# A fused attention and two MLPs on one core: the fixed order of the first batch written anew

## The chip, the cores and the metric

The kernel runs on one core of a Trainium2 chip. The metric is the device time of one execution in microseconds (us). "Before" is the kernel as it stood, "after" the kernel with the change.

## What is computed

The reference is an attention over pooled keys and values, and two MLPs behind it, all in float32:

```python
# q, k, v: (8, 8, 576, 64) = batch, heads, sequence, head size
k_p = k.reshape(B, H, 72, 8, D).mean(axis=3)      # 576 rows pooled to 72
v_p = v.reshape(B, H, 72, 8, D).mean(axis=3)
scores = scale * q @ k_p.T ; attn = softmax(scores)
x = (attn @ v_p) -> (4608, 512)                   # batch*sequence, heads*D
h = x @ w_in1 ; x = max(0.01*h, h) @ w_out1       # 512 -> 2048 -> 512
h = x @ w_in2 ; r = max(h, 0) ; out = (r*r) @ w_out2
```

The weights arrive as 64-bit floats, and the kernel decodes them itself from pairs of 32-bit words.

## The kernel before, in words

**Stages.** The first MLP runs over tiles of 512 tokens (`WIDE`, five of them) and 16 slices of 128 hidden columns; for each unit (tile t, slice f) `first` makes h = w_in^T x on PE and the activation, and `second` adds w_out^T g into four PSUM accumulators. Every operand of a product is split into a high and a low part (`hi` by a cast on ACT, `lo` by a subtraction on DVE), and three products take the place of one (`three`, lines 317 to 319). Behind that both MLPs go on in a scheme with fewer products (`first2`, `second2`), which the change does not touch.

**Attention beside the MLP.** `attention()` is a generator. Batch 0 is written out by hand in `first_batch`, since nothing can run beside it: the first MLP waits for its result. The other seven batches are stepped by `advance()`, some 2.5 steps a unit in the first tile and 5.25 later, so that they lie between the MLP's products.

**One batch.** The keys of 8 heads are loaded as 512 rows a head (`load_main`, 64 x 512 numbers a DMA; two tiles of 128 partitions, k_0 and k_2) and 64 more rows (`load_rest`, rk). `pooled` adds the 8 rows of a pool on DVE (line 356) or, for the batches in `K_ON_PE` and `V_ON_PE`, `pooled_pe` lets PE add them by products with the identity matrix (line 365: kp for keys, vp for values). `prepare_k` transposes the pooled keys on PE and copies them, scaled, into kT (ACT). `prepare_v` makes the values vM (high part on ACT, low part on DVE) and a block vR of the remaining rows, by way of GpSimd and six small DMAs (rx). The queries come in five chunks of up to 128 tokens, at 0, 128, 256 (64 wide), 320 and 448. For each chunk: `stage_a` transposes the queries (trq, PE) and copies them (qT, ACT). `stage_parts` makes the scores s (PE, line 554), their maxima mx (DVE, 564), eight exponentials x (ACT, 571), the sums' reciprocals rs (DVE, 584) and the products p (GpSimd, 586 and 593). `keys_part` and `rest_part` transpose p (pt, pr on PE), and `stage_d` makes the products o with the values, whose halves xh and xl are the MLP's input.

**Weights.** `fetch_weights` loads one slice (512 KB of w_in, 512 KB of w_out) into one of two staging buffers. `decode` turns it into floats in steps that share one buffer m: for slices 0 and 1 three operations on DVE (lines 205, 209, 212), one that puts in the sign (216), and a last one (226, an addition) that also waits for ACT's copy of the low words (225). For later slices ACT does the first (207). `split_weights` makes hl, high (ACT, 244) and low (DVE, 245).

**What sets the order.** In `first_batch` the lines q_in, a, b, c1, c2, d, w, fetch and next(pk), next(pv) emit the steps in the order in which each engine shall run them, and `in_order` fixes that order on each engine: no instruction there can pass the one ahead of it on its engine. a(i) is `stage_a` of chunk i; b(i) the next of the four parts of `stage_parts`; c1 and c2 are `keys_part` and `rest_part`; d(0) and d(4) one step of `stage_d` for the first 320 and the last 256 tokens; w(f) one step of decoding slice f. Behind h(0,0) the order is a scheduler's.

**Loads before.** ACT issues the four DMAs of k_0; SP issues rk, k_2, the queries of chunks 0 and 1, rv, the eight DMAs of the values, the queries of chunks 2 to 4, weight slice 0, rx, weight slice 1, and the queries and keys of batch 1.

**PSUM.** Four banks (`ps_w`) go round for trk, trq, vp, kp, pt, pr, o and h; the scores of batch 0 take the four banks of `ps_a` that are the MLP's accumulators later.

## Time and profile before

| | us |
|---|---|
| median of 3 runs (lowest, highest) | 1641.63 (1640.09, 1642.88) |
| the profiled execution | 1641.07 |
| its span, first to last instruction | 1639.3 |
| PE busy, share of the span | 1602.6, 98% |
| DVE busy | 1388.1, 85% |
| ACT busy | 1008.1, 61% |
| POOL busy | 117.3, 7% |

How to read the profile: PE is TensorE (PEld its loading of weights), DVE is VectorE, ACT ScalarE, POOL GpSimd, SP the engine that issues most DMAs; SPq and ACTq are issues of DMAs. Times count from the span's first instruction. A row of a timeline gives start, busy time, engine, line of the kernel, operation, "out<-in", and how often (x4); in brackets stands how long the engine was idle before it, and what ended that. A product of two float32 operands that are not split appears as two records.

### The profile page before, as it was taken

The numbers are of one execution on the slowest core, as the hardware profiler recorded it, in microseconds if no ns is written. First come the engines' busy times: TensorE is split into PE (matmuls) and PEld (weight loads), VectorE is DVE, ScalarE is ACT, GpSimd is POOL, SyncE is SP. The second block draws the span as 40 slices with busy tenths as digits, with TensorE's granted clock in tenths as the row PEclk, the third lists the DMA queues.
The fourth block names the chain that finished last, engine by engine and source line by source line (L and its number), as shares of the span: only waits on it lengthen the run. The fifth ranks groups of instructions, "written<-read, shape, count | busy, mean of one in ns | idle before, by whom it ended". The sixth has DMA issues, their size and how long they took to land.

```text
span 1639.3 us, 25990 instructions
## 1 busy us (share of the span) xinstructions
PE 1602.6 (98%) x9032; PEld 1466.8 (89%) x9032; DVE 1388.1 (85%) x2070; ACT 1008.1 (61%) x1930; POOL 117.3 (7%) x149
## 2 busy tenths in 40 slices
PE   5999999999999999999999999999999999999999
PEld 4877788888888999999999999998998998998997
DVE  6899776789889999979759589889789799799687
ACT  6777677755667867667557547456456455465454
POOL 4121222223110000000000000000000000000000
PEclk9999999999999999999999999999999999999999
DMA  8675554777547688887766764865865756756655
GB/s 212 190 203 169 144 134 139 233 217 224 180 157 257 244 284 296 265 304 231 225 190 204 236 186 151 281 196 149 275 187 176 254 177 198 241 171 209 196 167 167
DMA packets 223730, 340.94 MB, mean 208 GB/s; under 512 B 56176, under 2 KB 138096, under 8 KB 223600
## 3 DMA queue, kind: packets, MB, share of 16 engines
q1 hardware_dynamic: 223280, 338.76, 66.3%
q8 instruction: 72, 1.18, 0.3%
q10 hardware_dynamic: 320, 0.52, 0.1%
q14 instruction: 58, 0.48, 0.1%
HBM read 268.44 MB, written 69.21 MB: 206 GB/s over the span
## 4 chain that ended last, share of the span: by engine, by line
PE 83%; DVE 8%; ACT 4%; DMA 3%; issue 1%; SPq 0%; POOL 0%; ACTq 0%; DVEq 0%; POOLq 0%
PE psum L1078 14%; PE psum L317 14%; PE psum L319 14%; PE psum L318 14%; PE psum L1079 7%; PE h L317 3%; PE h L319 3%; PE h L318 3%; PE acc L318 3%; PE acc L319 2%; PE acc L317 2%; PE s L554 1%; ACT x L571 1%; DMA xs<-x 1%; DVE hl_out L245 1%
## 5 line engine op out<-in xcount | busy, mean ns | idle before, releaser
L1078 PE MATMUL psum<-wb_out,oh 128*128 128x512 f32 x1008 | 352.8, 394 | 0.0
L317 PE MATMUL psum<-xh,wb_in 128*128 128x384 f32 x1008 | 337.3, 335 | 2.2 <-ACT s L1052 1.2
L319 PE MATMUL psum<-xh,wb_in 128*128 128x384 f32 x1008 | 336.8, 334 | 0.0
L318 PE MATMUL psum<-xl,wb_in 128*128 128x384 f32 x1008 | 336.8, 334 | 0.0
L930 ACT CAST oh<-g 128x768 fp32r<-128x768 f32 x252 | 210.3, 836 | 160.1 <-PE psum L1078 89.3
L1079 PE MATMUL psum<-wb_out,ol 128*128 128x256 f32 x1008 | 281.8, 280 | 0.0
L931 DVE TENSOR_TENSOR ol<-g,oh 128x768 fp32r<-128x768 f32 x252 | 239.4, 954 | 17.4 <-ACT oh L930 14.9
L1078 PEld LDWEIGHTS psum<-wb_out,oh 128*128 128x128 f32 x1008 | 189.6, 188 | 43.1
L317 PEld LDWEIGHTS psum<-xh,wb_in 128*128 128x128 f32 x1008 | 189.2, 188 | 3.9 <-ACT s L1052 1.5
L318 PEld LDWEIGHTS psum<-xl,wb_in 128*128 128x128 f32 x1008 | 189.2, 188 | 0.2
L319 PEld LDWEIGHTS psum<-xh,wb_in 128*128 128x128 f32 x1008 | 189.2, 188 | 0.0
L1079 PEld LDWEIGHTS psum<-wb_out,ol 128*128 128x128 f32 x1008 | 188.8, 187 | 0.2
L984 ACT CAST wb_in<-wb_in 128x512 fp32r<-128x512 f32 x144 | 89.3, 621 | 146.4 <-DMA wb_in<-ws_in 141.4
L985 DVE TENSOR_TENSOR wb_in<-wb_in 128x512 fp32r<-128x512 f32 x144 | 98.7, 688 | 80.3 <-ACT wb_in L984 79.8
L934 DVE TENSOR_TENSOR g<-g,g 128x768 f32<-128x768 f32 x144 | 136.0, 952 | 1.5 <-ACT g L1006 1.0
L317 PE MATMUL h<-xh,hl_in 128*128 128x512 f32 (+1 forms) x320 | 121.8, 381 | 4.0 <-DVE pt_r L619 2.8
L317 PE MATMUL acc<-gh,hl_out 128*128 128x512 f32 (+1 forms) x320 | 120.2, 382 | 1.4 <-ACT hl_out L244 1.1
L318 PE MATMUL acc<-gl,hl_out 128*128 128x512 f32 (+1 forms) x320 | 118.6, 373 | 0.7 <-DVE gl L865 0.7
L319 PE MATMUL h<-xh,hl_in 128*128 128x512 f32 (+1 forms) x320 | 118.7, 371 | 0.0
L318 PE MATMUL h<-xl,hl_in 128*128 128x512 f32 (+1 forms) x320 | 118.1, 369 | 0.0
L319 PE MATMUL acc<-gh,hl_out 128*128 128x512 f32 (+1 forms) x320 | 117.9, 371 | 0.0
L318 PE MATMUL psum<-ol,wb_out 128*128 128x384 f32 x336 | 112.6, 335 | 0.0
(161 smaller groups left out, 3113.7 us busy)
## 6 DMA issues: line engine op xcount, KB each, us to landing
wb_in<-wd_in SPq DMA_DIRECT2D x108, 512.0 KB
wb_out<-wd_out SPq DMA_DIRECT2D x108, 512.0 KB
wb_in<-ws_in SPq DMA_DIRECT2D x144, 256.0 KB
wb_out<-ws_out SPq DMA_DIRECT2D x144, 256.0 KB
xs<-x SPq DMA_DIRECT2D x18, 768.0 KB
out_dram<-o SPq DMA_DIRECT2D x23, 384.0 KB
q<-in_q_dram SPq DMA_DIRECT2D x32, 256.0 KB
v<-in_v_dram SPq DMA_DIRECT2D x64, 128.0 KB
```

What stands on the lines that cost most here:

```text
L245: nc.vector.tensor_tensor(out=lo, in0=w, in1=raw(hi), op=ALU.subtract)
L317: nc.tensor.matmul(outp, ah, bh, start=first, stop=False, **kw)
L318: nc.tensor.matmul(outp, ah, bl, start=False, stop=False, **kw)
L319: nc.tensor.matmul(outp, al, bh, start=False, stop=last, **kw)
L554: nc.tensor.matmul(sc[:n, 2 * m:2 * m + 2].rearrange("p a x -> p (a x)"), qT[:, 2 * e + m, :n], kT[b % 2][:, 2 * e + m].rearrange("p a x - ...
L930: nc.scalar.copy(hi, src)
L931: nc.vector.tensor_tensor(out=lo, in0=src, in1=raw(hi), op=ALU.subtract)
L934: nc.vector.tensor_tensor(out=out_, in0=a, in1=b, op=ALU.subtract)
L984: nc.scalar.copy(whole[:, 0], raw(whole[:, 1]))
L985: nc.vector.tensor_tensor(out=whole[:, 1], in0=raw(whole[:, 1]), in1=raw(whole[:, 0]), op=ALU.subtract)
L1078: nc.tensor.matmul(outp, ah, b, start=first, stop=False, skip_group_check=True)
L1079: nc.tensor.matmul(outp[:, 1], al, b[:, 0], start=False, stop=last, skip_group_check=True)
```

## The change

- The first loads go over both issuing engines. ACT: both DMAs of the first half of the keys (`load_first`, 64 x 2 x 512 numbers each), the queries of chunks 0 and 1, both of the first half of the values. SP: the rest of the keys, the second half of the keys, weight slice 0, the rest and the second half of the values, the queries of chunks 2 to 4.
- The values of batch 0 are pooled by PE (vp) instead of DVE.
- The keys of batch 1 are loaded earlier, and their pooling by PE (kp) moves from behind h(0,0) to ahead of it; one PSUM bank stays with kp until ACT copies it, behind h(0,0).
- The decoding of weight slice 0 and most of slice 1 moves ahead of parts of the attention.
- The transposes and copies of the first keys are made half by half.
- For the batches from 1 on, the pooling of the last rows of keys (`pool_rest`) stands behind kp.

```diff
--- before.py
+++ after.py
@@ -56,7 +56,7 @@
     RG = KR * H // 2
     SPANS = (320, 256)
     EARLY = 5
-    V_ON_PE = (1,)
+    V_ON_PE = (0, 1)
     K_ON_PE = (1,)
     AHEAD = 5
     RATES = (2.5, 5.25)
...
+            def load_first(src, nm, issue):
+
+                ts = []
+                for g in range(2):
+                    ts.append(kv_tile(0, P, 2, f"{nm}0_{g}"))
+                    heads = src[0, 4 * g:4 * g + 4, 0:KM * POOL, :].rearrange(
+                        f"({'a r' if nm == 'k' else 'r a'}) (kk j) d -> a kk r (j d)", a=2, j=POOL
+                    )
+                    for a in ((0, 1), (1, 0))[g]:
+                        issue[g].dma_start(out=ts[g][a * KM:(a + 1) * KM], in_=heads[a])
+                return ts
+
+            def load_rest(b, src, nm):
...
             def load_k(b):
-                if b < B:
-                    both = [nc.scalar, nc.sync] if b == 0 else [nc.sync, nc.sync]
+                if b == 0:
+                    KV["k", b] = load_rest(b, k, "k"), load_first(k, "k", [nc.scalar, nc.sync])
+                elif b < B:
                     KV["k", b] = (
-                        load_rest(b, k, "k", both[1]),
-                        load_main(
-                            b, k, "k", [[4 * (m // 2) + m % 2 + 2 * a for a in range(2)] for m in range(NP)], both
-                        ),
+                        load_rest(b, k, "k"),
+                        load_main(b, k, "k", [[4 * (m // 2) + m % 2 + 2 * a for a in range(2)] for m in range(NP)]),
                     )
 
             def load_v(b):
+                if b == 0:
+                    KV["v", b] = load_rest(b, v, "v"), load_first(v, "v", [nc.scalar, nc.sync])
+                    return
                 KV["v", b] = (
                     load_rest(b, v, "v"),
...
             def prepare_k(b):
                 kr, kk = KV.pop(("k", b))
                 i = b % 2
                 kd = ap1.tile([P, NP, D], F32, tag="kd", name=f"kd{b}")
                 rr = ap1.tile([KR * H, 2, D], F32, tag="rr", name=f"rr{b}")
-                pooled(rr[:, 0:1], kr)
-                nc.vector.tensor_copy(rr[:, 1], rr[:, 0])
+
+                def pool_rest():
+                    pooled(rr[:, 0:1], kr)
+                    nc.vector.tensor_copy(rr[:, 1], rr[:, 0])
+
+                if b == 0:
+                    pool_rest()
+                    tr = work("trk0")
+                    for g in range(2):
+                        pooled(kd[:, 2 * g:2 * g + 2], kk[g])
+                        turned(tr, kd, g)
+                        if g == 0:
+                            turned_rest(tr, rr)
+                            put_rest(i, tr)
+                        put_keys(i, tr, slice(2 * g, 2 * g + 2))
...
+                    return
                 if b in K_ON_PE:
                     for ps in pooled_pe(f"kp{b}", kk):
                         yield
+                    pool_rest()
                     nc.scalar.copy(kd, ps)
                 else:
+                    pool_rest()
                     for m in range(0, NP, 2):
                         pooled(kd[:, m:m + 2], kk[m // 2])
-                        if b > 0:
-                            yield
-                            continue
-                        tr = work("trk0") if m == 0 else tr
-                        nc.tensor.transpose(
-                            tr[:, m * D:(m + 2) * D], kd[:, m:m + 2].rearrange("p a d -> p (a d)"), ident
-                        )
                         yield
-                if b > 0:
-                    load_v(b)
-                    tr = work(f"trk{b}")
-                for g in range(2 if b > 0 else 0):
-                    nc.tensor.transpose(
-                        tr[:, g * P:(g + 1) * P], kd[:, 2 * g:2 * g + 2].rearrange("p a d -> p (a d)"), ident
-                    )
-                nc.tensor.transpose(
-                    tr[:, 2 * P:2 * P + KR * H], rr.rearrange("p a d -> p (a d)"), ident[:KR * H, :KR * H]
-                )
-                for r in range(2):
-                    rows = slice(r * D, (r + 1) * D)
-                    nc.scalar.activation(
-                        kT[i][rows, :, r, 0:KM], tr[rows, 0:2 * P].rearrange("p (m x) -> p m x", x=KM),
-                        AF.Copy, scale=scale / POOL,
-                    )
-                    nc.scalar.activation(
-                        kT[i][rows, :, r, KM:SP],
-                        tr[rows, 2 * P:2 * P + KR * H].rearrange("p (m r x) -> p m r x", r=2, x=KR)[:, :, r],
-                        AF.Copy, scale=scale / POOL,
-                    )
...
-            def load_q(b, span, at, off, n):
+            def load_q(b, span, at, off, n, issue=None):
                 qn[b, at] = qp.tile([P, H, D], F32, tag="q", name=f"q{b}_{at}", bufs=3)
-                nc.sync.dma_start(out=qn[b, at][:n], in_=q[b, :, at:at + n, :].rearrange("h p d -> p h d"))
...
+            pk1 = []
+
             def first_batch():
-                pk, pv = prepare_k(0), prepare_v(0)
...
                     stage_a(*chunks[i])
@@ -696,78 +737,81 @@
                     RAW[f] = fetch_weights(1, [("in", f), ("out", f)])
 
                 load_k(0)
-                q_in(0)
-                q_in(1)
+                q_in(0, nc.scalar)
+                q_in(1, nc.scalar)
+                fetch(0)
                 load_v(0)
+                pk, pv = prepare_k(0), prepare_v(0)
                 q_in(2)
                 next(pk)
                 a(0)
                 next(pk)
-                next(pk)
                 a(1)
                 q_in(3)
                 q_in(4)
-                fetch(0)
-                next(pv)
-                fetch(1)
                 b(0)
                 b(0)
                 b(1)
+                next(pv)
+                fetch(1)
+                load_k(1)
+                pk1.append(prepare_k(1))
+                b(0)
+                b(1)
+                w(0)
+                w(0)
+                next(pv)
+                next(pv)
+                a(2)
                 b(1)
                 b(0)
-                next(pv)
-                b(1)
-                b(0)
-                a(2)
-                next(pv)
-                b(1)
-                a(3)
+                w(0)
                 b(2)
                 b(2)
                 next(pv)
+                a(3)
                 b(2)
-                b(2)
-                c1(0)
+                b(1)
+                w(0)
                 b(3)
                 b(3)
+                c1(0)
                 c2(0)
+                b(3)
+                b(2)
+                a(4)
+                b(4)
+                b(4)
                 c1(1)
                 c2(1)
                 next(pv)
-                a(4)
+                b(4)
+                b(3)
+                w(1)
+                w(1)
+                split_weights("in", 0, 0)
+                fetch(2)
+                c1(2)
+                c2(2)
+                b(4)
+                next(pk1[0])
+                d(0)
+                d(0)
+                d(0)
+                d(0)
+                w(1)
                 q_in(5)
                 q_in(6)
                 q_in(7)
-                load_k(1)
-                c1(2)
-                c2(2)
-                b(3)
-                b(4)
-                b(4)
-                w(0)
-                b(3)
-                d(0)
-                d(0)
-                b(4)
-                w(0)
-                b(4)
-                d(0)
-                d(0)
-                w(0)
-                w(0)
-                fetch(2)
                 c1(3)
                 c2(3)
+                next(pk1[0])
                 c1(4)
                 c2(4)
-                split_weights("in", 0, 0)
-                w(1)
-                w(1)
                 d(4)
                 d(4)
                 d(4)
                 d(4)
-                w(1)
                 w(1)
                 first(0, 0)
                 fetch(3)
@@ -783,7 +827,7 @@
             marks.append(in_order(first_batch))
             ready[0] = 1
             yield
-            yield from prepare_k(1)
+            yield from pk1[0]
             stage_b(*chunks[nch])
             yield
             def finish(i):
```

Where the order moves, on the engines that the prediction speaks of. In these rows a name ends in the chunk's first token and a running number; s, mx, x, qT, trq are the scores, maxima, exponentials and transposed queries of a chunk.

ACT, from the first exponentials on, before:

```order
L571 ACTIVATE x_0_279,sm_0_280<-s_0_0_282,mx_0_0_288 128x72 x4
L571 ACTIVATE x_0_279,sm_0_280<-s_0_1_285,mx_0_1_290 128x72 x4
L571 ACTIVATE x_128_292,sm_128_293<-s_128_0_295,mx_128_0_301 128x72 x4
L571 ACTIVATE x_128_292,sm_128_293<-s_128_1_298,mx_128_1_303 128x72 x4
L537 COPY qT_256_335<-trq_256_330 128x4x64
L537 COPY qT_320_351<-trq_320_346 128x512
L500 ACTIVATE vM_181<-vd_262 64x4x64 x2
```

and after:

```order
L611 ACTIVATE x_0_256,sm_0_257<-s_0_0_259,mx_0_0_265 128x72 x4
L611 ACTIVATE x_0_256,sm_0_257<-s_0_1_262,mx_0_1_267 128x72 x4
L577 COPY qT_256_345<-trq_256_340 128x4x64
L611 ACTIVATE x_128_269,sm_128_270<-s_128_0_272,mx_128_0_314 128x72 x4
L611 ACTIVATE x_128_269,sm_128_270<-s_128_1_275,mx_128_1_316 128x72 x4
L540 ACTIVATE vM_181<-vp_323 64x4x64 x2
L577 COPY qT_320_384<-trq_320_379 128x512
L611 ACTIVATE x_256_362,sm_256_363<-s_256_0_365,mx_256_0_371 64x72 x4
L611 ACTIVATE x_256_362,sm_256_363<-s_256_1_368,mx_256_1_373 64x72 x4
L225 ACTIVATE w_0_318<-st_in_out_203 128x1024
L645 CAST pt_h<-pt_0_415 128x4x128
```

The copy qT_256 has moved between the exponentials of chunks 0 and 1, qT_320 stays behind them and behind vM, which is now made from vp; the copy for weight slice 0 (w_0) comes ahead of pt_h.

PE, behind the scores of chunks 0 and 1, before (trq_256 is the transposes of q_256):

```order
L554 MATMUL s_0_1_285<-kT_179,qT_0_237 128x144 x2
L554 MATMUL s_128_0_295<-kT_179,qT_128_253 128x144 x2
L554 MATMUL s_128_1_298<-kT_179,qT_128_253 128x144 x2
L533 MATMUL trq_256_330<-ident,q_256_219 128x64 x4
L533 MATMUL trq_320_346<-ident,q_320_255 128x128 x4
L554 MATMUL s_256_0_356<-kT_179,qT_256_335 64x144 x2
```

and after:

```order
L594 MATMUL s_128_0_272<-kT_179,qT_128_250 128x144 x2
L594 MATMUL s_128_1_275<-kT_179,qT_128_250 128x144 x2
L365 MATMUL vp_323<-v_0_208,ident 128x128 x8
L365 MATMUL vp_323<-v_1_211,ident 128x128 x8
L573 MATMUL trq_256_340<-ident,q_256_214 128x64 x4
L594 MATMUL s_256_0_365<-kT_179,qT_256_345 64x144 x2
```

The pooling of the values, vp, stands between the scores and trq_256.

PE, ahead of the last products of the attention (o_1), after; before, kp stands behind the first products of h_0_1 instead:

```order
L678 MATMUL o_0_3_550<-pt_r,vR 128x320
L644 MATMUL pt_320_564<-ident,p_320_485 128x128 x4
L656 MATMUL pr_320_571<-ident,p_320_485 96x128 x2
L365 MATMUL kp_520<-k_2_301,ident 128x128 x8
L644 MATMUL pt_448_584<-ident,p_448_514 128x128 x4
L656 MATMUL pr_448_591<-ident,p_448_514 96x128 x2
L317 MATMUL o_1_0_596<-pt_h,vM_181 128x256
```

The second half of kp stands ahead of the transposes pt_448.

DVE, around the last decode step of slice 3 and the first of slice 4, behind h(0,0), before:

```order
L216 SCALAR_TENSOR_TENSOR wm_3_666<-st_in_out_634,wm_3_666 128x1024
L356 TENSOR_TENSOR rr_710<-rk_436 64x64
L226 ISA w_3_665<-wm_3_666,w_3_665 128x2048
L428 COPY rr_710<-rr_710 64x64
L209 TENSOR_SCALAR wm_4_677<-wm_4_677 128x1024
L212 TENSOR_SCALAR wm_4_677<-wm_4_677 128x1024
L356 TENSOR_TENSOR rv_749<-rv_749 64x256
```

and after (rv, rd and mx belong to batch 1):

```order
L216 SCALAR_TENSOR_TENSOR wm_3_689<-st_in_out_657,wm_3_689 128x1024
L474 COPY rr_519<-rr_519 64x64
L356 TENSOR_TENSOR rv_737<-rv_737 64x256
L226 ISA w_3_688<-wm_3_689,w_3_688 128x2048
L356 TENSOR_TENSOR rv_737<-rv_737 64x128
L604 TENSOR_REDUCE mx_0_0_782<-s_0_0_776 128x4
L356 TENSOR_TENSOR rd_884<-rv_737 64x64
L604 TENSOR_REDUCE mx_0_1_784<-s_0_1_779 128x4
L209 TENSOR_SCALAR wm_4_700<-wm_4_700 128x1024
```

The rest of the second values and the first maxima of batch 1 have come ahead of L209 of slice 4.

## Rows read from the trace of the kernel before

**Rows 1.** The page, part 1: engine, busy us (share of the span), instructions.

```profile
PE 1602.6 (98%) x9032; PEld 1466.8 (89%) x9032; DVE 1388.1 (85%) x2070; ACT 1008.1 (61%) x1930; POOL 117.3 (7%) x149
```

**Rows 2.** Windows: stretch, length, PE, PEld, DVE, ACT, POOL busy, PEclk, DMA share, GB/s.

```profile
0.00:5.00 5.00, 0.00 (x0) 0.00 (x0) 0.38 (x1) 1.49 (x2) 4.34 (x13) 1.00 0.50 139
5.00:10.00 5.00, 0.58 (x3) 0.61 (x4) 2.82 (x9) 0.00 (x0) 0.00 (x0) 1.00 1.04 226
10.00:15.00 5.00, 4.86 (x20) 3.76 (x19) 2.04 (x7) 2.60 (x9) 1.26 (x1) 1.00 0.84 221
15.00:20.00 5.00, 3.06 (x18) 2.48 (x18) 3.84 (x10) 5.00 (x32) 0.80 (x1) 1.00 1.15 282
20.00:25.00 5.00, 5.00 (x28) 4.34 (x26) 3.78 (x10) 3.80 (x20) 3.48 (x6) 0.66 0.90 274
...
40.00:45.00 5.00, 4.95 (x20) 4.47 (x21) 4.87 (x10) 2.66 (x9) 0.00 (x0) 0.61 0.35 118
```

**Rows 3.** Timeline of ACT, 14 to 22 us.

```profile
14.49 0.32 ACT L571 ACTIVATE x<-s,mx 128x72 f32<-128x72 f32 x1 [1.34 <-DVE mx L564]
...
19.25 0.95 ACT L537 COPY qT<-trq 128x256 f32<-128x256 f32 x2
...
21.35 0.85 ACT L500 ACTIVATE vM<-vd 64x256 fp32r<-64x256 f32 x2 [1.15 <-DVE vd L356]
```

**Rows 4.** Timeline of PE, the last products o_1 and the first of h(0,0).

```profile
42.76 0.41 PE L318 MATMUL o<-pt_l,vM 128*128 128x256 f32 x1
42.98 0.41 PE L319 MATMUL o<-pt_h,vM 128*128 128x256 f32 x1
...
43.64 0.63 PE L317 MATMUL h<-xh,hl_in 128*128 128x512 f32 x1
```

**Rows 5.** Windows behind h(0,0), and the longest wait of PE in them.

```profile
44.00:76.00 32.00, 30.59 (x175) 25.17 (x175) 28.60 (x45) 25.06 (x54) 1.66 (x2) 1.00 0.66 198
76.00:110.00 34.00, 31.23 (x158) 25.34 (x156) 32.95 (x54) 27.43 (x70) 9.15 (x10) 1.00 0.75 218
110.00:152.00 42.00, 39.03 (x191) 31.55 (x191) 41.27 (x63) 32.78 (x79) 7.40 (x7) 1.00 0.58 168
...
92.79 0.47 PE L317 MATMUL h<-xh,hl_in 128*128 128x512 f32 x1 [2.77 <-DVE pt_r L619]
```

**Rows 6.** Timeline of SP's issues: weight slice 0.

```profile
15.07 0.83 SPq L191 DMA_DIRECT2D st_in_out<-in_moe_w_in_dram  x1
15.95 0.50 SPq L196 DMA_DIRECT2D st_in_out<-in_moe_w_out_dram  x1
```

**Rows 7.** Timeline of PE, transposes of queries and scores.

```profile
11.41 1.11 PE L533 MATMUL trq<-ident,q 128*128 128x128 f32 x4
12.66 4.14 PE L554 MATMUL s<-kT,qT 128*128 128x144 f32 x16
16.73 0.46 PE L533 MATMUL trq<-ident,q 64*128 64x64 f32 x4
17.52 0.63 PE L533 MATMUL trq<-ident,q 128*128 128x128 f32 x4 [0.32 <-DMA q<-in_q_dram]
```

**Rows 8.** Timeline of PE, pooling by products: half of kp, all of vp, batch 1.

```profile
56.03 1.95 PE L365 MATMUL kp<-k,ident 128*128 128x128 f32 x16
...
72.87 3.84 PE L365 MATMUL vp<-v,ident 128*128 128x128 f32 x32 [0.43 <-ACT x L571]
```

**Rows 9.** Timeline of DVE: decode steps of slices 0 and 4.

```profile
36.96 1.23 DVE L226 CUSTOM_DVE_ANT_0 w<-wm,w 128x2048 uint16<-128x2048 uint16 x1
...
61.55 0.69 DVE L209 TENSOR_SCALAR wm<-wm 128x1024 f32<-128x1024 f32 x1 [1.10 <-ACT wm L207]
```

**Rows 10.** DMA queues between 2 and 6 us: packets, MB, share (q10 is ACT's).

```profile
q10 hardware_dynamic: 298, 0.49, 42.6%
q1 hardware_dynamic: 266, 0.46, 42.4%
```

More of the change, by code (lines that the diff above doesn't have):

```diff
@@ L418, in load_v, with turned, turned_rest, put_keys @@
                 )
+            def turned(tr, kd, g):
+                nc.tensor.transpose(
+                    tr[:, g * P:(g + 1) * P], kd[:, 2 * g:2 * g + 2].rearrange("p a d -> p (a d)"), ident
+                )
+            def turned_rest(tr, rr):
+                nc.tensor.transpose(
+                    tr[:, 2 * P:2 * P + KR * H], rr.rearrange("p a d -> p (a d)"), ident[:KR * H, :KR * H]
+                )
+            def put_keys(i, tr, ms):
+                for r in range(2):
+                    rows = slice(r * D, (r + 1) * D)
+                    nc.scalar.activation(
+                        kT[i][rows, ms, r, 0:KM], tr[rows, 0:2 * P].rearrange("p (m x) -> p m x", x=KM)[:, ms],
+                        AF.Copy, scale=scale / POOL,
+                    )
+            def put_rest(i, tr):
+                for r in range(2):
+                    rows = slice(r * D, (r + 1) * D)
+                    nc.scalar.activation(
+                        kT[i][rows, :, r, KM:SP],
+                        tr[rows, 2 * P:2 * P + KR * H].rearrange("p (m r x) -> p m r x", r=2, x=KR)[:, :, r],
+                        AF.Copy, scale=scale / POOL,
+                    )
             def prepare_k(b):
@@ L660, in attention, with q_in @@
             nch = len(chunks) // B
+            pk1 = []
             def first_batch():
-                pk, pv = prepare_k(0), prepare_v(0)
                 part = [None] * nch
                 dec, rows = {}, {}
-                def q_in(i):
-                    load_q(*chunks[i])
+                def q_in(i, issue=None):
+                    load_q(*chunks[i], issue)
                 def a(i):
```

17 lines of the change are left out of this document (12 added, 5 removed).

## Prediction

> **What bounds the kernel now.** I read the page first, then the windows, the timelines of ACT, PE, SP and DVE over the first 50 us, and the windows behind them. PE is busy 98% of the span and DVE 85% [rows 1], so a part of the program can only gain where PE does not already work without a break, and that is the beginning. In the first 25 us the DMA engines are what works: their share is 1.04, 0.84, 1.15 and 0.90 in the four windows from 5 us on, and only the first window, at 0.50, has room [rows 2]. ACT takes over from there. It starts on the exponentials of chunk 0 at 14.49 and has finished those of chunks 0 and 1 when it copies qT_256 and qT_320 at 19.25, so 16 exponentials with their read-outs take 4.76 us, 2.38 a chunk. At 20.20 both copies are done, and at 21.35 ACT has waited 1.15 us for the pooled values [rows 3]. The first MLP product, h(0,0), starts on PE at 43.64 [rows 4]. From there to about 152 us DVE is the tight engine: 28.60 of 32, 32.95 of 34 and 41.27 of 42 us, while PE leaves 1.4, 2.8 and 3.0 us idle and once waits 2.77 us for a DVE result [rows 5]. What moves the end is therefore the start of h(0,0), and behind it DVE's work.
>
> **The sum goes against the profiled execution's 1641.07 us**, which is 0.56 below the median of the runs shown, 1641.63; 0.2% is 3.3 us, about what a measurement of this kernel can tell from no change.
>
> **Step 1, the loads.** The megabyte of weight slice 0 (two issues of 512 KB, 0.83 and 0.50 us of SP's time [rows 6]) moves from behind q_448 to ahead of the last 64 rows and of half of the values. Everything behind it on SP, that is rv, v_1 and q_256 to q_448, lands later. I count bytes at the rates of the first windows [rows 2]: 0.70, 1.83, 2.93 and 4.34 MB have moved by 5, 10, 15 and 20 us. The values need 0.13 + 1.05 + 0.52 + 0.13 + 1.05 = 2.88 MB before the change (rest of the keys, keys, q_0 and q_128, rest of the values, values) and 3.93 MB after it, which is 15 + 1.00 / 0.282 = 18.5 us. Before, DVE could take the values at 17 us without a wait. A landing is later than the count: q_320 is due at 16.2 by it (3.28 MB) and PE waits for it until 17.52 [rows 7], 1.3 us more. I take 0.7, so v_1 at 19.2, with 18.5 and 19.8 as ends.
>
> That the loads go over two queues I price at nothing. By the windows alone [rows 2] a second queue could at most fill the first 5 us to the rate of the next 5: (226 - 139) x 5 us = 0.43 MB, or 1.6 us less of lag; from 5 us on no DMA time is free. I take none of it, since the first window also holds the start, when nothing has been issued yet. The Trainium skill has a rule on this in "DMA: Bandwidth & Descriptors", section "Issuing engines are not separate DMA queues": transfers started by different engines run on the same 16 DMA engines, and a second issuer saves only the time of issuing. By that rule the gain is nothing as well, where the row's upper end is 1.6 us.
>
> **Step 2, what waits for them.** In the new PE order the pooling of the first values (vp) stands ahead of the transposes trq_256, and in ACT's order qT_256 still stands ahead of the exponentials of chunk 1. So a late v_1 holds back q_256, and through it ACT, with everything that ACT has queued. The 32 records of one vp take 3.84 us [rows 8]; the second half, 16, comes behind v_1: 19.2 + 1.92 = 21.1. The transposes take 0.46 [rows 7], the copy 0.48 (half of 0.95 [rows 3]): 22.05. The exponentials of chunk 1 take 2.38: 24.4; qT_320, which is not yet copied then, 0.48: 24.9. Before, the same state is reached at 20.20. **Lag: 4.7 us.** Low end 4.0, with v_1 at 18.5. High end 6.8: v_1 at 19.8 and PE at the slower of its levels, at which four transposes took 1.11 instead of 0.63 [rows 7], so 3.4 for the half vp. The second values issue on ACT sits ahead of the first kT copies; it costs one issue (0.5 to 0.8 [rows 6]) in a stretch where ACT waits for q_0 anyway: nothing.
>
> **Step 3, from there to h(0,0).** ACT has the same operations in both orders, so only waits count. The 1.15 us for the values on ACT [rows 3] go, since vp is then long done. The last 16 products of the attention (o_1) ran at a granted clock of 0.61 in their window [rows 2], one per 0.22 us [rows 4], the pace of 1.2 GHz; with the key pooling kp ahead of them PE has work there, and at 2.4 GHz the 16 take half of their 3.5 us: -1.75. Against it, the second half of kp, 16 records and 1.95 us [rows 8], stands ahead of pt_448 in PE's queue, and every later product waits for that: +1.95 (0 if PE would have waited for GpSimd there anyway). And the maxima of chunk 320 now stand in DVE's queue behind the last decode step of slice 0 (1.23 us [rows 9]), which waits for ACT's copy: +1.2 (0 if ACT gets there early). -1.15 - 1.75 + 1.95 + 1.2 = **+0.25**; ends -2.9 and +3.15.
>
> **Step 4, behind h(0,0).** kp's 32 records leave the MLP's stretch: 3.9 us less for PE. I count that at nothing, because DVE is the tight engine there: PE's wait of 2.77 us for DVE [rows 5] becomes longer by what PE saves. DVE's own work behind h(0,0) stays: the decode step of slice 1 that now comes earlier ends in a wait for the first gl. What PE's lead buys is that DVE finds the rest of the second values and the first maxima of batch 1 ready where it waited 1.10 us for ACT [rows 9]: **-1.1**, with 0 as the other end. Pooling the first values on PE takes two v poolings from DVE, in the stretch where ACT is the bound: nothing.
>
> 4.7 + 0.25 - 1.1 = +3.85 us: 1644.9 on the profiled execution, **1645.5** against the median. The forecast's own range is 1642.5 to 1649.
>
> **Rivals.**
> *The weights starve the small pieces* (slower still). While both queues move pieces of 2 KB they share evenly, 298 packets of one and 266 of the other between 2 and 6 us [rows 10]. q_0 and q_128 come in pieces of 256 bytes and would meet the weights' pieces of 1 and 4 KB. If the queues take turns by piece, SP's queue is through before q_128 is: 3.41 MB, 16.7 + 0.7 = 17.4 us. Then the chain from q_128's transposes to the last score, 11.41 to 16.80 [rows 7], ends at 22.8, vp at 26.6, qT_256 at 27.6, and with 2.86 more the state of 20.20 comes at 30.4: lag 10.2, so 1651. The skill's same page, section "Queues, rings and completion order", says that an engine goes round its queues packet by packet, which would be this case; with equal pieces [rows 10] it can't be told from sharing by bytes. Chance 0.15.
>
> *PE counts behind h(0,0)*. If DVE's order, not its amount of work, makes PE's waits there [rows 5], PE's 3.9 us come off: 1641.6. For it: PE is busy 30.59 of 32 us in the first of these windows. Against it: DVE is nearly without a gap in the next two. Chance 0.17.
>
> *The loads are not late* (faster). The first 5 us have a DMA share of 0.50 [rows 2]; four large issues in place of eight could fill it. It decides if v_1 is there by 14.5 us, so that half a vp and the transposes are done when chunk 0's exponentials end at 16.9. Then there is no lag, slice 0 is decoded early, kp hides in waits for GpSimd: -2.9 - 1.1 = -4.0, 1637.6. Against it: a full first window gives the 1.6 us of step 1, not 4.7; it would need a fuller use later too. Chance 0.20.
>
> **How the numbers follow.** The forecast has 0.48. Faster by over 0.2% means under 1638.4: most of the third rival and a little of the second, 0.17. Slower by over 0.2% means over 1644.9: more than half of the forecast's range, the first rival, 0.46. The rest, 0.37. The range runs from 1638.4, which leaves out the better part of the third rival, to 1650.5.
>
> **What would show it.** Right: ACT waits 3 us or more ahead of qT_256; trq_256 comes after 20 us, behind vp, whose second half waits for a DMA; h(0,0) starts near 48.5; PE's idle time between h(0,0) and 110 us behind it grows by about kp's 3.9 us; the granted clock is 1.00 in the window of o_1. Wrong: exponentials of chunk 0 after 17 us (first rival); h(0,0) at 48.5, yet a time near 1641 (second); qT_256 before 18 us and h(0,0) before 43 (third).

## The result, and the profile after

| | before | after |
|---|---|---|
| median, us (4 runs each, same chip) | 1642.26 | 1665.38 |
| lowest, highest | 1640.09, 1644.78 | 1662.40, 1666.34 |
| the profiled execution, its span | 1641.07, 1639.3 | 1664.83, 1663.1 |
| start of h(0,0) in the profile | 43.64 | 64.41 |
| from there to the end of the span | 1595.7 | 1598.7 |

The ratio is 1.0137, 95% interval [1.0117, 1.0157]: some 22 us slower. Of the 23.8 us between the two profiles 20.8 lie ahead of h(0,0) and 3.0 behind it.

The page of after, part 1, and the windows of the beginning (columns as in [rows 1, 2]):

```profile
PE 1612.4 (97%) x9064; PEld 1478.0 (89%) x9064; DVE 1383.1 (83%) x2064; ACT 1008.7 (61%) x1932; POOL 117.6 (7%) x149
```
```profile
0.00:5.00 5.00, 0.00 (x0) 0.00 (x0) 0.00 (x0) 0.00 (x0) 4.36 (x13) 1.00 0.53 117
5.00:10.00 5.00, 0.74 (x2) 0.36 (x2) 2.51 (x7) 0.51 (x1) 0.00 (x0) 1.00 1.17 170
10.00:15.00 5.00, 1.45 (x5) 0.90 (x5) 1.41 (x3) 2.26 (x7) 0.00 (x0) 1.00 1.13 290
15.00:20.00 5.00, 0.15 (x1) 0.00 (x0) 0.00 (x0) 0.72 (x3) 0.00 (x0) 1.00 1.07 193
20.00:25.00 5.00, 4.19 (x20) 4.20 (x21) 1.52 (x4) 2.18 (x12) 0.00 (x0) 1.00 0.67 147
...
45.00:50.00 5.00, 4.86 (x25) 4.27 (x24) 3.85 (x7) 4.63 (x22) 2.62 (x3) 0.50 0.38 60
50.00:55.00 5.00, 3.26 (x13) 2.91 (x13) 3.55 (x8) 0.72 (x3) 3.00 (x5) 0.50 0.01 2
55.00:60.00 5.00, 5.00 (x30) 4.94 (x29) 3.56 (x6) 1.93 (x5) 0.12 (x1) 0.64 0.00 0
60.00:65.00 5.00, 4.21 (x28) 3.34 (x27) 2.24 (x6) 2.50 (x10) 0.00 (x0) 1.00 0.06 13
```

From 15 to 20 us, where ACT had no gap before, every engine nearly stands (ACT 0.72 us busy, PE 0.15) and the transfers run at a share of 1.07. The timelines of ACT, then of PE, show what stood for what (they answer to [rows 3, 4, 7, 8]):

```profile
23.41 0.32 ACT L611 ACTIVATE x<-s,mx 128x72 f32<-128x72 f32 x1 [0.87 <-DVE mx L604]
...
29.26 0.37 ACT L577 COPY qT<-trq 128x256 f32<-128x256 f32 x1 [3.32 <-PE trq L573]
...
33.26 0.59 ACT L577 COPY qT<-trq 128x512 f32<-128x512 f32 x1
...
39.13 0.32 ACT L611 ACTIVATE x<-s,mx 128x72 f32<-128x72 f32 x1 [1.13 <-DVE mx L604]
...
41.52 0.62 ACT L577 COPY qT<-trq 128x512 f32<-128x512 f32 x1
45.37 0.59 ACT L645 CAST pt_h<-pt 128x512 fp32r<-128x512 f32 x1 [3.23 <-PE pt L644]
```
```profile
12.97 1.12 PE L573 MATMUL trq<-ident,q 128*128 128x128 f32 x4 [3.52 <-DMA q<-in_q_dram]
...
20.81 1.11 PE L573 MATMUL trq<-ident,q 128*128 128x128 f32 x4 [5.66 <-DMA q<-in_q_dram]
...
25.04 3.73 PE L365 MATMUL vp<-v,ident 128*128 128x128 f32 x32
28.71 0.46 PE L573 MATMUL trq<-ident,q 64*128 64x64 f32 x4
...
42.19 2.29 PE L594 MATMUL s<-kT,qT 128*128 128x144 f32 x8 [4.64 <-ACT qT L577]
...
46.73 3.78 PE L365 MATMUL kp<-k,ident 128*128 128x128 f32 x16
...
52.52 0.64 PE L318 MATMUL o<-pt_l,vM 128*128 128x320 f32 x1 [1.74 <-DVE pt_l L646]
...
53.22 0.47 PE L678 MATMUL o<-pt_r,vR 96*128 96x320 f32 x1
...
64.05 0.28 PE L318 MATMUL o<-pt_l,vM 128*128 128x256 f32 x1
...
64.41 0.40 PE L317 MATMUL h<-xh,hl_in 128*128 128x512 f32 x1
```

The first exponential starts at 23.41 instead of 14.49. PE waits 3.52 us for q_0 and 5.66 us for q_128, whose transposes start at 20.81 instead of 11.41. vp behind them doesn't wait for the values: its 32 records run on from 25.04. Then there is a second row of waits, from 36 to 46 us: qT_448 is copied behind the exponentials of chunk 320, PE waits 4.64 us for it, and ACT then 3.23 us for PE. DVE stands in the same stretch (timeline of DVE, answering to [rows 9]):

```profile
37.30 1.23 DVE L226 CUSTOM_DVE_ANT_0 w<-wm,w 128x2048 uint16<-128x2048 uint16 x1 [3.18 <-ACT w L225]
...
43.55 0.46 DVE L604 TENSOR_REDUCE mx<-s 128x4 f32<-128x288 f32 x1 [2.72 <-PE s L594]
```

Behind h(0,0) the windows at about the same distance from it as in [rows 5], and PE's longest wait there:

```profile
64.00:97.00 33.00, 28.87 (x157) 23.79 (x158) 29.17 (x47) 28.02 (x72) 4.71 (x5) 1.00 0.74 210
97.00:131.00 34.00, 31.56 (x148) 24.85 (x147) 31.90 (x54) 25.76 (x67) 8.53 (x10) 0.95 0.70 205
131.00:173.00 42.00, 38.72 (x185) 31.68 (x184) 40.46 (x61) 32.77 (x67) 4.26 (x5) 0.96 0.59 182
...
105.78 0.50 PE L319 MATMUL h<-xh,hl_in 128*128 128x512 f32 x1 [2.44 <-DVE hl_in L245]
```

PE has 4.1 us idle in the first of them, where it had 1.4 in 32 us. Last, the DMA queues of after from 7 to 13 us, then its first and its last two us, 7 to 9 and 11 to 13 (packets, MB, share of 16 engines; q10 is ACT's queue, answering to [rows 10]):

```profile
q1 hardware_dynamic: 678, 0.83, 65.8%
q10 hardware_dynamic: 1545, 0.39, 54.4%
...
q10 hardware_dynamic: 578, 0.15, 75.0%
q1 hardware_dynamic: 85, 0.15, 51.6%
...
q1 hardware_dynamic: 447, 0.49, 87.2%
q10 hardware_dynamic: 389, 0.10, 27.2%
```

From 7 to 13 us ACT's queue, with the queries, and SP's, with the weights, have nearly the same share of the engines' time, but SP's moves twice the bytes. That is a mean of unlike stretches: from 7 to 9 us both move 0.15 MB, from 11 to 13 us SP's moves 0.49 MB and ACT's 0.10.

### The profile page after: what moved, and what is told of

Same layout as the page of the kernel before. It is cut to its first block, busy times and chain, and to the rows that moved or that the text cites. A ratio compares the mean times of both kernels' runs of the same rounds, so it can differ in the third digit from the quotient of the medians.

```text
span 1663.1 us, 26023 instructions
## 1 busy us (share of the span) xinstructions
PE 1612.4 (97%) x9064; PEld 1478.0 (89%) x9064; DVE 1383.1 (83%) x2064; ACT 1008.7 (61%) x1932; POOL 117.6 (7%) x149
## 4 chain that ended last, share of the span: by engine, by line
PE 84%; DVE 7%; ACT 4%; DMA 3%; issue 1%; SPq 0%; ACTq 0%; DVEq 0%
PE psum L1122 14%; PE psum L317 14%; PE psum L319 14%; PE psum L318 14%; PE psum L1123 7%; PE h L319 3%; PE h L317 3%; PE h L318 3%; PE acc L317 3%; PE acc L318 3%; PE acc L319 3%; PE s L594 2%; ACT x L611 1%; DMA q<-in_q_dram 1%; DMA wb_in<-ws_in 1%
```

## The experiments

All eighteen in one table. Ratios are to the kernel before on the same chip (medians of before 1639.8 to 1642.0 us in the experiments). The last two columns are of one profiled execution of each kernel, and they vary between executions: e8 and e13 have the same program ahead of h(0,0), and it starts at 46.94 and 50.95; so have the change and e14 (64.41 and 62.67), e9 and e16 (48.66 and 49.43), before and e17 (43.64 and 43.82). So a difference of one to four us in these columns is not settled by two traces alone. Nor is every profiled execution a typical one: that of e1 took 1663.60 us, the longest of its four, that of e8 1650.79, the shortest of its five.

| run | ratio [95%] | median | h(0,0) | behind it |
|---|---|---|---|---|
| the change | 1.0137 [1.0117, 1.0157] | 1665.38 | 64.41 | 1598.7 |
| e1_q_on_sp | 1.0128 [1.0113, 1.0143] | 1660.01 | 58.17 | 1603.6 |
| e2_weights_late | 1.0143 [1.0126, 1.0160] | 1663.30 | 58.77 | 1602.3 |
| e3_old_loads | 1.0113 [1.0098, 1.0128] | 1658.49 | 58.07 | 1597.5 |
| e4_new_loads | 1.0041 [1.0026, 1.0056] | 1646.54 | 49.24 | 1595.7 |
| e5_decode_late | 1.0093 [1.0076, 1.0110] | 1656.98 | 52.91 | 1603.4 |
| e6_decode_keys_late | 1.0079 [1.0064, 1.0094] | 1654.41 | 52.13 | 1600.5 |
| e7_only_values | 1.0036 [1.0025, 1.0048] | 1647.26 | 47.12 | 1598.8 |
| e8_only_keys | 1.0075 [1.0060, 1.0090] | 1653.65 | 46.94 | 1602.1 |
| e9_query_early | 1.0076 [1.0061, 1.0091] | 1653.38 | 48.66 | 1601.5 |
| e10_values_and_keys | 1.0078 [1.0065, 1.0091] | 1655.03 | 48.44 | 1601.8 |
| e11_keys_back | 1.0061 [1.0048, 1.0073] | 1650.94 | 52.38 | 1596.5 |
| e12_filler_before | 1.0014 [1.0005, 1.0023] | 1644.27 | 44.45 | 1595.0 |
| e13_keys_paced | 1.0020 [1.0011, 1.0030] | 1645.52 | 50.95 | 1592.8 |
| e14_change_paced | 1.0122 [1.0108, 1.0136] | 1663.07 | 62.67 | 1598.5 |
| e15_values_queries | 1.0026 [1.0015, 1.0037] | 1646.66 | 44.72 | 1598.7 |
| e16_mended | 1.0045 [1.0031, 1.0058] | 1649.16 | 49.43 | 1597.5 |
| e17_pace_only | 1.0007 [0.9998, 1.0016] | 1642.38 | 43.82 | 1596.9 |
| e19_keys_in_gaps | 1.0005 [0.9995, 1.0014] | 1641.14 | 43.44 | 1595.7 |

### Loads or order

e1 and e2 move loads back within the change; e3 gives the new order the old loads; e4 gives the old order the new loads. S stands for small pieces starved on ACT's queue, W for the weights' bytes, O for the new order losing by itself.

```diff
-q_in(0, nc.scalar); q_in(1, nc.scalar); fetch(0)    # the change
+q_in(0); q_in(1); fetch(0)                           # e1
+q_in(0, nc.scalar); q_in(1, nc.scalar)               # e2: fetch(0) behind q_in(4)
```

> The change, but the queries of chunks 0 and 1 are issued by SP, behind the second half of the keys and ahead of weight slice 0; everything else as changed. Theory S (pieces of 256 bytes on ACT's queue lose against pieces of 1 to 4 KB on SP's, because the DMA engines take turns by piece): q_128 is there by 12 us instead of 20.8, the first exponential starts near 15 us instead of 23.4, and some 9 us of the 23 come back, so about 1654 to 1657. Theory W (the early megabyte of weights holds everything back by its bytes): little changes, 1662 or more, since the weights still stand ahead of the values and of q_256. Theory O (the new order of the computation loses the time by itself): the first exponential is early, but the time stays above 1660.

> The change, but weight slice 0 is loaded behind the queries of chunk 4, as before; the queries of chunks 0 and 1 stay on ACT. Theory S: q_0 and q_128 now share the engines with 2 KB pieces of the values on SP only: q_128 comes at 14 to 16 us, the first exponential at 17 to 19, time 1650 to 1656. Theory W: all of the loss on the load side goes, q_128 by 12 us, first exponential near 15, time 1645 to 1650. Theory O: as the change, above 1660.

> The change's order of the computation with the loads exactly as before (first half of the keys on ACT, all else on SP, weight slice 0 behind the queries). Theory S or W: the first exponential is back at 14.5 us, h(0,0) starts at 42 to 46 us, time 1638 to 1645. Theory O: h(0,0) above 50 us and a time above 1650 although all loads are on time.

> The order of the computation as before, with the change's loads (two queues, weight slice 0 early). Theory S or W: first exponential near 23 us as in the change, and a time 10 to 20 us above before, 1652 to 1662. Theory O: within 4 us of before. S and W alone are not told apart by this run.

e4 stands by itself: all the change's loads together cost 5.6 us of h(0,0) in the old order, and behind it nothing is added or given back (timeline of PE in e4; before, the first of these rows was at 11.41). Its time, 1646.54, lies between the ranges of S or W and of O:

```profile
17.44 1.12 PE L550 MATMUL trq<-ident,q 128*128 128x128 f32 x4 [3.76 <-DMA q<-in_q_dram]
...
49.24 0.80 PE L317 MATMUL h<-xh,hl_in 128*128 128x512 f32 x1
```

Neither S nor W gave its range of time in any of the four. In e2 the landings came where S puts them: q_128's transposes start at 14.75 and the first exponential at 17.35. So without the early weights the change's loads make q_128 3.3 us later than before, and the early weights 6.1 us more; yet the time of e2, 1663.30, is that of the change (timeline of PE in e2):

```profile
14.75 1.11 PE L573 MATMUL trq<-ident,q 128*128 128x128 f32 x4 [1.61 <-DMA q<-in_q_dram]
```

In e1 the queries come early and the first exponential starts at 13.94, but now the values are behind the weights, and of the 9.5 us gained by then 5.6 are waited away at qT_256, which is copied at 25.36 instead of 29.26 (timelines of ACT and of PE in e1):

```profile
13.94 0.32 ACT L611 ACTIVATE x<-s,mx 128x72 f32<-128x72 f32 x1 [0.87 <-DVE mx L604]
...
25.36 0.37 ACT L577 COPY qT<-trq 128x256 f32<-128x256 f32 x1 [8.88 <-PE trq L573]
```
```profile
19.37 5.50 PE L365 MATMUL vp<-v,ident 128*128 128x128 f32 x32 [4.46 <-DMA v<-in_v_dram]
```

O was right in e3, but e3 and e2 can't tell more: with the weights late, the decoding that the change puts early stands in DVE's order and waits for them, a wait that the experiment itself made (timeline of DVE in e3; 3.81 us in e2):

```profile
22.89 0.69 DVE L205 TENSOR_SCALAR wm<-st_in_out 128x1024 uint32<-128x1024 uint32 x1 [7.05 <-DMA st_in_out<-in_moe_w_out_dram]
```

### Which part of the order

e5 is e3 with the decoding of slices 0 and 1 (all w(0), w(1) and the split of in-slice 0) at the places of before. e6 also moves the keys back, e7 and e8 are single parts of the change put into before.

```diff
-V_ON_PE = (1,)
+V_ON_PE = (0, 1)                 # e7, on before
+load_k(1); pk1 = prepare_k(1)    # e8, on before: behind fetch(1)
+next(pk1)                        # e8: ahead of d(0), and between c2(3) and c1(4)
```

> The change's order of the first batch with the loads of the kernel before, and in addition the decoding of weight slices 0 and 1 (and the split of in-slice 0) back at the places of the kernel before. Three theories of what the new order loses (with the old loads and the early decode it stood 18.5 us above before, and VectorE stood 7.05 us at L205 for the weights). D, the decoding steps stand too early in VectorE's and ScalarE's order and hold what the softmax needs: under 4 us above before. P, TensorE's pooling of the first values and second keys stands ahead of what is waited for, and runs in part at the low clock: 8 us or more above before. I, the interleaving of the chunks' steps itself loses: 8 us or more above before.

> As the run with the late decoding, and the pooling of the second batch's keys back behind the first MLP of batch 0 as well. D: under 4 us above before, and within 2 us of the run with the late decoding alone. P: at least 4 us faster than the run with the late decoding alone. I: 8 us or more above before, and within 2 us of the run with the late decoding alone.

> The kernel before with one edit: the first batch's values are pooled by TensorE. D and I: within 2 us of before on either side. P: 3 us or more slower than before, by 32 matmuls of 3.84 us ahead of the third and fourth query transposes.

> The kernel before with one edit: the second batch's keys are loaded behind the second weight slice and pooled by TensorE in two steps ahead of the first MLP, at the two places that the change gives them. D and I: within 2 us of before on either side. P: 3 us or more slower than before, by 3.9 to 5.8 us of TensorE ahead of the outputs of the first attention span.

D falls: with the decoding late (which P and I both allow) the change's order is still 15 us above before, and either pooling alone is slower than before by 5.9 and 12.3 us. e6 is a miss, because the load of the keys was put behind q_5 to q_7: its nine issues (rk, and k eight times) then stand on SP right ahead of the stores of xo, and ACT waits for those 7.09 us (timeline of ACT in e6):

```profile
59.54 0.21 ACT L686 COPY xo<-o 128x64 f32<-128x64 f32 x1 [7.09 <-DMA x<-xo]
```

Before, ACT copied qT_256 and qT_320 together; in e7 half of vp stands between their transposes (timeline of ACT):

```profile
21.88 0.58 ACT L537 COPY qT<-trq 128x512 f32<-128x512 f32 x1 [2.05 <-PE trq L533]
```

In e8 kp waits for the keys and holds o_0 back, and its sums keep one of the four banks, so that pr_320 waits until DVE has read an o_0; before has no such wait, and e19 (below), whose sums lie in another bank, has none either. Behind h(0,0) PE waits for gh, 3.34 us at once, where before has 0.2 us of such waits (timeline of PE in e8):

```profile
30.19 2.02 PE L365 MATMUL kp<-k,ident 128*128 128x128 f32 x16 [1.17 <-DMA k<-in_k_dram]
...
37.31 0.40 PE L616 MATMUL pr<-ident,p 128*96 128x128 f32 x2 [2.15 <-DVE xl L648]
...
112.09 2.08 PE L317 MATMUL acc<-gh,hl_out 128*128 128x512 f32 x4 [3.34 <-ACT gh L869]
```

### The fifth chunk's queries, the sum of the parts, and the clock

```diff
 b(3); b(3)
+a(4)                             # e9, on e5: transposes and copy of qT_448
 c1(0); c2(0); b(3); b(2)         # this b(3) is the exponentials of chunk 320
-a(4)
```

e10 is e8 with e7's line. e11 is e5 with the keys' pooling behind h(0,0) and their load, with q_5 to q_7, behind a(4). e12 is before with idle products of `ident` by `ident` ahead of the transposes of the fourth and fifth chunk.

> As the run with the late decoding (17.2 us above before), and the transposes and the copy of the queries of the fifth chunk (qT_448) back ahead of the exponentials of the fourth (x_320). Two theories of what is left. Q, that copy's place behind eight exponentials breaks the overlap of the two chunks (TensorE stood 3.17 us for ScalarE's qT, ScalarE 3.23 us for TensorE's pt, one behind the other): 3.5 us or more faster than the run with the late decoding alone. P, the two poolings on TensorE are the price, each by its own: within 2 us of that run.

> The kernel before with both poolings at once: the first values by TensorE and the second keys ahead of the first MLP. It has the order of the chunks and the loads of before. P: the sum of the two single runs, 7.5 + 13.9 = 21 us above before, and at least 16. Q: 3.5 us or more faster than the run with the late decoding, which differs by the order of the chunks alone, so 13.7 us above before or less.

> As the run with the late decoding, with the pooling of the second keys back behind the first MLP and their load back at the place of before (behind the transposes of the fifth chunk, so that the stores of the first output tile don't queue behind it). P: at least 6 us faster than the run with the late decoding alone. Q: within 3 us of it, as the pooling lies in time in which TensorE stands for qT_448 in any case.

> The kernel before, with 30 idle matmuls of 128x128 added (results overwritten) where TensorE stands for the weights' softmax of the fourth and fifth chunk, from 31.8 to 38.5 us. C, the low clock is a price of its own in the first batch: the outputs of the second span run at the full clock (16 matmuls at some 0.12 us apart and not 0.21), 1 us or more faster than before. Not C: within 1 us of before, or slower by what the fillers hold up, 0 to 2 us.

In e9 h(0,0) comes 4.25 us earlier than in e5; the time falls by 0.0017 of before, 2.8 us, short of Q's 3.5, and the intervals overlap; e16, with the same program ahead of h(0,0), has it at 49.43, 3.5 us earlier than e5. The wait is gone, as these rows show (timeline of ACT in e5, then in e9):

```profile
30.46 0.61 ACT L577 COPY qT<-trq 128x512 f32<-128x512 f32 x1
...
34.30 0.59 ACT L645 CAST pt_h<-pt 128x512 fp32r<-128x512 f32 x1 [3.23 <-PE pt L644]
```
```profile
26.98 0.58 ACT L577 COPY qT<-trq 128x512 f32<-128x512 f32 x1 [0.41 <-PE trq L573]
```

e10 falls in Q's range of time above before: the two poolings together cost 12.8 us and not 18. That they share their waits was not tried by itself; against e5 it is 2.5 us by the ratios, and the intervals overlap. e11 is between the theories, 5.3 us faster than e5, and in the profiles nearly all of that is behind h(0,0): 1596.5 instead of 1603.4. So in this order the early keys cost mostly where work was taken away.

e12 answers for the clock of o_1 in the order of before. The o_1 products run at 2.4 GHz with the fillers (0.28 us each, where [rows 4] have 0.41, granted clock 1.00 in place of 0.61), and h(0,0) is still not earlier, since it waits for DVE; the whole is 0.0014 of before slower, 2.3 us, with the fillers (timeline of PE in e12):

```profile
42.74 0.28 PE L645 MATMUL o<-pt_r,vR 96*128 96x256 f32 x1
44.45 0.50 PE L317 MATMUL h<-xh,hl_in 128*128 128x512 f32 x1 [1.43 <-DVE xl L655]
```

### The steps behind

When the two pooling steps of batch 1's keys are taken out of the attention's later steps, the loop over the MLP's slices, which takes 2.5 steps a slice, comes to every later step two steps sooner. Two empty steps undo that shift and nothing else:

```diff
+yield
+yield
 yield from pk1[0]
```

e13 is e8 with them, e14 the change, e16 is e9; e15 is e7 with a(3) ahead of the second half of vp.

> As the run with the keys alone (12.3 us above before), and two empty steps at the place behind the first batch where the two pooling steps stood in the kernel before. The loop over the MLP's slices takes 2.5 steps of the attention a slice, so that without the empty ones each later step comes two steps nearer to the start. N, this shift of the steps is the price behind the first MLP (6.4 of the 9.7 us that the run with the keys alone was longer in its profile): 4 to 8 us faster than that run. R, the price there lies in the pooling itself or its place on TensorE: within 2 us of that run.

> The whole change, and the two empty steps at the same place. N: 1 to 5 us faster than the change (whose profile was 3.0 us longer than before behind the first MLP). R: within 1 us of the change.

> As the run with the values alone (5.9 us above before), and the transposes and the copy of the queries of the fourth chunk (qT_320) ahead of the second half of the pooling, so that ScalarE makes both copies together as in the kernel before. Q, ScalarE's wait of 2.05 us for that copy started the delay: 3 us or more faster than the run with the values alone, and perhaps faster than before, as VectorE has 6.6 us less to do. P, the pooling on TensorE is the price by itself: within 2 us of that run.

> The change's order with the loads of before, the decoding late, the queries of the fifth chunk early (12.5 us above before so far), and the two empty steps. N: 4 to 8 us faster than that run without the empty steps, 4.5 to 8.5 us above before. R: within 2 us of that run.

N holds where the keys are early: e13 is 0.0055 of before faster than e8 (9 us, a little above its range), e16 0.0031 faster than e9 (5 us), each with intervals apart. e13's profile even has 2.9 us less than before behind h(0,0), though its own keys came late (kp waited 2.57 us and ran 3.75 us, where e8's ran 2.02), and h(0,0) starts at 50.95. In the whole change the step of 2.5 us lies within the intervals and behind h(0,0) nothing moved (1598.5); there N is not shown. In e15 ACT's wait for trq_320 is gone and h(0,0) is 2.4 us earlier than in e7, the time 1.6 us, within the intervals.

The last two ask whether the shift costs by itself, and whether early keys can pay at all. e17 has the two empty steps in before. e19 puts next(pk1) ahead of c1(3) and between c2(3) and c1(4), kp into an accumulator bank, the remainder's pooling behind, and the two empty steps.

> The kernel before with the two empty steps alone, behind its own pooling of the second keys, so that each later step of the attention comes two steps further from the start. N, the place of the steps against the MLP's slices is a price in both directions: over 2 us slower or faster than before. If only coming nearer costs (two steps nearer cost some 6 us in the run with the keys alone): within 2 us of before.

> The kernel before with the second keys pooled early in another way than the change: the two pooling steps stand where TensorE waits for GpSimd's p (ahead of the transposes of the fourth chunk, and between those of the fourth and the fifth), their sums lie in one of the four accumulator banks and not in the transposes' banks, the remainder keys are pooled behind, and the two empty steps keep the later ones in place. If the change's places were the fault (kp waited 1.17 to 2.57 us for the keys and held the first outputs, and took one of four banks): the first MLP within 1 us of before, and 1 to 4 us faster than before in all, as 4 us of TensorE leave the later stretch. If early keys don't pay at all: within 1 us of before, or slower.

Both are level with before; for e17 that is the sign that only coming nearer costs. In e19 kp costs nothing ahead of h(0,0), since it stands in time in which PE waited for GpSimd (timeline of PE):

```profile
31.44 1.95 PE L365 MATMUL kp<-k,ident 128*128 128x128 f32 x16
...
34.26 2.02 PE L365 MATMUL kp<-k,ident 128*128 128x128 f32 x16
...
43.44 0.58 PE L317 MATMUL h<-xh,hl_in 128*128 128x512 f32 x1
```

And the 4 us that PE no longer has to do behind it don't shorten that stretch: 1595.7 as before. No version here beats before.

## Why the prediction was wrong

The direction was right, the size was not: 3.85 us forecast, 22 to 24 found.

**Step 1 and 2, the loads and their lag.** The shape holds: ACT waits 3.32 us ahead of qT_256, trq_256 comes behind vp, after 20 us. The cause does not: vp never waits for the values, so the late v_1, from which the step counts its whole chain, held nothing. What came late was q_128. The state that stood at 20.20 is reached at 33.85, so the lag is 13.65, not 4.7. Two things failed. Bytes were counted for the values alone, with the queries of chunks 0 and 1 taken as punctual, yet these were late: in the old order the change's loads together move h(0,0) by 5.6 us (e4), and with these queries back on SP's queue it comes 6.2 us earlier than in the change (e1). In e1 the wait of the forecast is there: vp waits 4.46 us for the values. And *that the loads go over two queues I price at nothing* failed on the other side of the range I gave it: it could lose. By the Trainium skill ("DMA: Bandwidth & Descriptors", "Issuing engines are not separate DMA queues") a second issuer brings only issue time, and the trace agrees that nothing was gained: 117 GB/s in the first 5 us, where before had 139. The order between the loads, which a single queue kept in e1 (q_0 and q_128 transposed at 10.22 and 11.34), was lost.

**The first rival** had the right sign (first exponentials after 17 us: 23.41) and a lag of 10.2 of the 13.65, with a chance of 0.15. Its ground, turns by piece, is not shown: that would be as many packets of the profile from either queue, and from 7 to 13 us there are 1545 of q10 to 678 of q1. The Trainium skill ("DMA: Bandwidth & Descriptors", "Queues, rings and completion order") says that an engine goes round its queues packet by packet; but its packet is a run of typically 9 to 17 descriptors, not one of the pieces that the profile counts, so turns by piece don't follow from it, and no run here tests it. The third rival, loads not late, is refuted by the same rows.

**Step 3, from that state to h(0,0)**, was +0.25 and is 33.85 to 64.41, 30.56 instead of 23.44: +7.1. The sentence that failed is *ACT has the same operations in both orders, so only waits count*: I did not compare their order. qT_448 went behind eight exponentials, the next scores wait for it, the next exponentials for those: 4.25 us of h(0,0) between e5 and e9. kp's second half was priced at 1.95 with its wait for GpSimd as cover; its first half, ahead of o_0, and the bank that it keeps, were not priced. With both poolings e9 is still 5.0 us late at h(0,0), and e10, in the old chunk order, 4.8. The +1.2 for the maxima behind the last decode step is there as 1.13 us of ACT's wait at 39.13.

The -1.75 for the clock of o_1 is there in the rows (granted clock 1.00, 0.28 us each). What it was worth in the change is not shown: in e12 h(0,0) waits for DVE in any case, while in the change it follows the last o_1 without a gap. The clock of o_0 was not priced, and there it cost: the o_0 of after run one per 0.27 us at a granted clock of 0.50, the 1.2 GHz level, those of e1 one per 0.15 us (a row of e1's timeline of PE, then a window of e1). From the second o_0 to the transposes pt_448 after needs 7.6 us (52.52 to 60.08), e14 7.5 and e1 5.2, with the same operations. Ahead of these products PE had stood 4.64 and 1.74 us in after and nearly as long, 4.29 and 1.75, in e1; why the clock rose earlier in e1 is not shown.

```profile
50.16 0.31 PE L319 MATMUL o<-pt_h,vM 128*128 128x320 f32 x1
...
50.00:55.00 5.00, 4.66 (x37) 3.99 (x35) 4.05 (x7) 2.65 (x7) 1.23 (x3) 1.00 0.01 2
```

**In one chain**, by the start of h(0,0): 6.2 us for the queries on ACT's queue (the change to e1), of which 3.9 stand ahead of the second o_0 and 2.4 come behind it with the lower clock; 5.3 for the rest of the loads with the early decoding (e1 to e5); 4.25 for the place of qT_448 (e5 to e9); 5.0 for the two poolings and what else is left of the new order (e9 to before): 20.8. Each is one pair of traces; with e14 in place of the change the first is 4.5. The second is several edits. e3 has these loads with the early decoding and stands at 58.07, as e1 does, so what they are worth shows only together with the late decoding.

The measured ratios give other weights in the same order: the queries 0.0009 of before (1.5 us, within the intervals), the other loads with the decoding 0.0035 (5.7 us), qT_448 0.0017 (2.8 us, the intervals overlap), then the two empty steps 0.0031 (5 us, e9 to e16), and 0.0045 (7.4 us) that e16 still has above before. Shown clear of the intervals are the second, the empty steps and the rest that e16 keeps.

**Step 4, behind h(0,0)**, was -1.1 and is +3.0. That kp's 3.9 us are worth nothing there fits e19 (1595.7 in both), so the second rival finds no support there; the 1592.8 of e13, where h(0,0) came late, leaves a rest open. PE's idle time in the three windows grew from 7.2 to 9.9 us, less than the 3.9 of the sign. What was missed is that steps taken out of a list that is served at a fixed rate bring all later ones nearer: shown in e13 and e16. In the change itself the 3.0 stay open, e14 did not move them. The granted clock of after fell to 0.95 and 0.96 in windows where it was 1.00 before. In the first of these PE waits 2.44 us (105.78); whether the clock costs by itself there was not tried.

Open as well: e1 has h(0,0) 6.2 us earlier than the change and gains 1.5 us of time by the ratios, 3.1 by the medians. Its profile has 1603.6 behind h(0,0), but of an execution 3.6 us above its median, so how much is lost there, and why, was not isolated.

## What to carry to other kernels

When an order is written anew, compare the order of the *dependent* operations on each engine, not their number: by the start of h(0,0), one copy that moved behind eight exponentials cost about as much as a whole pooling by products. A load that moves to another queue must be priced in both directions, because it gives up its place ahead of what the other queue carries. And work taken out of a paced list shifts the rest of the list; put an empty step in its place before judging the move.

## What was not expected of the hardware

Two queues that were both at work shared the DMA engines by no single rule that these rows show. Over 6 us their shares of the engines' time were near each other, 54.4% and 65.8%, at 1545 packets to 678; but within it the bytes were equal from 7 to 9 us (0.15 MB each), and from 11 to 13 us the packets nearly were (389 and 447). In the mean of the 6 us a packet of about 250 bytes took some 34 ns of an engine (an estimate, 0.544 x 16 x 6 us / 1545), one of about 1.2 KB some 93 ns (0.658 x 16 x 6 us / 678); as the two shares add up to more than 1, packets overlap on an engine, and these are not times that it gave to one alone. Over the 6 us the small pieces got the worse of it by bytes, 0.39 MB to 0.83.

A stretch of TensorE at 1.2 GHz ahead of a wait for VectorE gained nothing when it was lifted to 2.4 GHz (e12). A stretch on the path, with no such wait behind it, took 7.6 us instead of 5.2 (the change and e1).
